# Ten warm-up operations for twelve, the layernorm's shift in one VectorE operation, and a new order table

## The chip, the cores and the metric

The kernel runs on one core of one Trainium2 chip. A core has five engines that work side by side, each with an instruction queue of its own: TensorE (PE; its weight loads are listed as PEld), VectorE (DVE), ScalarE (ACT), GpSimd (POOL) and SyncE (SP), which here issues nearly all transfers. The metric is the device time of one execution in microseconds, as a median of runs.

## The reference

Four residual blocks follow each other: attention, MLP, attention, MLP. S is 2048, D is 512, 32 heads of 16 columns, a sliding window of 256 keys, F is 1792.

```python
def _A_ref(x, wqkv, wo):                       # x already layernormed
    q, k, v = ...                              # x @ wqkv, 32 heads of 16
    scores = einsum("bhqd,bhkd->bhqk", q, k) * (Dh ** -0.5)
    scores = where((q_idx - k_idx >= 0) & (q_idx - k_idx < 256), scores, -1e9)
    return reshape(einsum("bhqk,bhkd->bhqd", softmax(scores), v)) @ wo

def _B_ref(x, w1, b1, w2, b2):                 # mixes along the tokens
    h = _layernorm(x)
    u = gelu(einsum("bsd,sf->bdf", h, w1) + b1)
    return transpose(einsum("bdf,fs->bds", u, w2) + b2)

x = A_x
x = x + _A_ref(_layernorm(x), A_wqkv, A_wo)
x = x + _B_ref(_layernorm(x), B_w1, B_b1, B_w2, B_b2)
x = x + _A_ref(_layernorm(x), A_wqkv, A_wo)
x = x + _B_ref(_layernorm(x), B_w1, B_b1, B_w2, B_b2)
```

## The kernel before

Everything stays in SBUF in bf16: x as 16 tiles of 128 tokens by 512 columns (`x_sb`), its normalised copy (`xh_sb`), and k, v and q of the stretch in work. A layer's attention runs over four quarters Q of 512 queries; in each, over four groups t of eight heads, and in each of these over nine steps m. A step multiplies q by k into two PSUM banks (`emit_scores`, L797), takes the exponential on ScalarE (L808), masks the edges of the window on VectorE or POOL (L825), and multiplies by v into banks 4 and 5 (`emit_pv`, L846). Between the steps stand the jobs that feed them: transposes of normalised tiles into `xhT` (L569, L582), projections for k, q (L593) and v (L697, turned on VectorE at L700, spread at L712 or L717), evacuations of PSUM by `copy_out` (L442 on VectorE, L444 on ScalarE), and the output projection (L762), after which x is added and its statistics are taken (L766, L527, L528). The MLP follows: L609 (parts made ahead, beside attention) and L987 with the gelu at L994, then L1033 with the sum at L1037. Banks 6 and 7 serve all these jobs in turn.

`ln_stats` (L526) takes mean and variance of a tile. `ln_apply` (L530) makes the normalised tiles from them, mostly four tiles at once: `vare`, the variance plus epsilon (L537, VectorE); `rstd`, its power -1/2 (L539, POOL); `nmean`, the mean times -1 (L541, VectorE); `shift`, `nmean` times `rstd` (L543, POOL); and per tile x times `rstd` plus `shift` (L546 on VectorE or POOL, L549 on ScalarE). There are 17 such calls: two of two tiles at the start, and 15 of four.

The start: four loads of one x tile, then the weights; on POOL the identity matrix, the triangle `tri` and some constants; on VectorE the mask `edge`, eight small pieces made from `tri` (L490, L492), the columns `half` and `even`; three zero fills of `q_sb` (L495) on VectorE or POOL. Meanwhile TensorE multiplies the identity by itself, twice in a warm-up operation (L521), into banks 4 and 5. Then tiles 0 to 3 are normalised, transposed, and multiplied into the first k, q and v. wv is also reordered in halves (`permute_wv`, L686 to L688).

The order of every engine is fixed beforehand. Each operation is registered with the engines that could take it, a priority and an estimate of its duration. A planner, `arrange`, could order them by these, but it isn't called as long as `LINES` is there: `given` takes each engine's list of operation numbers from that table, and with it the choice of engine. `ORDER` sets in which order the jobs are registered, and so who waits for whom; `BANKS` says which of banks 6 and 7 a job takes. An engine works its list strictly in order, and a wait at its head holds all behind it:

```python
    def emit(self, block):
        line = self.line = self.given() if LINES else self.arrange()
...
                    for k, (sem, val) in waits.items():
                        if seen.get(k, 0) < val:
                            seen[k] = val
                            e.wait_ge(sem, val)
                    o.on[ename][1](e).then_inc(o.mark[0], 16 if o.dma else 1)
```

Of the kernel before, what the change touches and what calls it, by code (L numbers as in the profile page):

```python
# [14 lines left out]
WARM = 12  # L15
# [14 lines left out]
def _table(*text):  # L30
# [5 lines left out]
    'c-pO%NfLlC2n6Z*|D!$VA(pZwQ02iO5IRgWGvj$=s}a1_t)7LW%>DZDUfy1PqA2I%kl8c?b5B|cGg6XlcP%#(x1TjeVa`gOe{yPcK<L$?wAm@}'  # L36
    'VkysiU77XM`Cn79HbaE`*=AYKIH|352Ds;6D^<qc%}i^DBpz)O@D)yLnj()z{$97jIlPxA?E)0O0EP')
ORDER = _table(
    'c-jTQ17HvU00h8C*0OEeT()i7ww7(%wr$(CZSxKgh_DC-BLspY6ao+$$q^f25FX(W5)ly<5fB5B5g(Bd577||DG(D$5C;hn7YPsz8ITC6kqn8E'
    '6xp#48IclckPoSl4QY`HMUW1eksDc%9t{u$Igu4PPyl6+7rBrJg^?eDD2O^JijpXV;;4dRD31~-h0<t`%BYC4D2FDfh6<>ON~nr%sE*pGfm*1C'  # L40
    'uIPhCXo~unfVyaohG>jd7>O2WgJx)nb{K?CXpOe$fR5;lE|`lR=!Ny@hwd1Np6H8F7=XbThHVH!e+<QNOha#sz!)6D5RAuYjKeI9#bivyOiaWi'
    'Ou=-_!3@mCJj};gEW`pV#R)9OA}ql&ti&p;zz3|w2JFTfY{EKh#8xcE4s5}8?7~hw#%0{a9_+_Ktj1m(z-HXT5gf)boWe((!BL#YN!-9C9LH&#'
    '!$n*Lc?B164cGAlw{R1;aR+hu0Qd0-uka90@dPjM9Ix>b&+rzB_y+Is4quR*pYR=@@eO|vnqL9_#xI!v@E2kThGZIsWf(?aAWJYZgE2fKF)G6`'
    'fH7Esu^5HX8J9m1it!nfu^EpE8Jr22go&Ay$(WJRn35@&nyHwU*_e(Q7?GKoo|%}HjhKZwn4P(pn|V2ytyq)!nUjT>hxu5LMOc)DS%Ae^ip5xl'
    'l~|r7S(T+(ku_L_)mWC5S&Ow<opo8C^;m}u*?>*ioNd^WP1u3W*qWW$j&0eVo!F5**o{5ei(T1;ec7A+*^gs6h{M>J137|2IGm$6n%y~plNiLI'
    'oXU|L&xstv>72r8oW<E3$C;eRxm>{cT*yUS#-&`z6<ovRoWnlc#?{=-bzIMD+`!3P!d+a<jl9gOyuwx7#GAa%&Ai1M+`{eL!L8iMJ>1Lv+{cqV'
    '!Bf1z(>%^&yvU<G$0Iz$!#u!)Jj+8o&-=W@+q}a^e9Gs1$9sIhXMD&f{K&g}%ny9cmwdw)e8snX&)@vaPyE7f45LW;&Y%2B3;Mx7{L7U3MJc!v'
    '=pRFh3awxYp->8^hzhF+3a`wHtf-2q=n7C2MN@1QR9wYUd^J)WB~c=kR&~WwLZwk+C07d7Rc@tMDrHn!^-)%3S4(A3E@e?R<y2nfQGVr90Zmp1'
    '1*)*Rsf-G#go>+_%Bj36sfvOWL)BDKHC0(vRYSE@TlLjYO_Wac)LadeT8-6AEtE;EltanXRPEG8om5h-)m3d(K^@gaWz|!iRZRU<RK3+h1Jz4|'
    ')mOtbK!Y??b<|!XHA15_R!cQn<FsEhH9_MwMUym7(==7nHACGsOS3gs{k2eYG+&FgM9XwktF%%pv|KwiTx+yi>oi6iwN@LnS?je;o3vFsG*R2N'  # L50
    'OIx%@yR}ybbWlfhSjTlpr*uN6bxy~0QfG8t7j;3G^iEH;NY`~)w{=6ebWL}3RrmBn4|P`dO+D8GJ<=Op(FfhvK0Vemeb!sO)_eWXC;ie_z0`O8'
    '(@%ZTU(tVbS1<HR!3@hG9MT^Z%Ap<H-}GDI9N;((ba+R0SVwaNM{-0*bxg;0DJODVM{#_|a6;#B7{_uF$8!QFcVZ`VN~dyCr*L$qab;(87N>So'
    'cXd{0a4u(dI%ju!_jev=b0ODuPUm(}7jy|1aWQ9d8K-qg=XC{_c6nEHK38%z7jR+Ma9P)NRTp;^S9cvZa6>nC6PI&KH+O5davQgEdv|ax_iz{2'
    'bA5MmH#c%m_jNP(a$65}9}jepTX=*Ad6<WKxJP@G$9s%BySFF0pT~KEC%L<)d9tT_fM<E8XLzpXc)pkWh>v-J7kagidaB2Ih}ZbAr+ATPdx=l@'
    'lo$J?k9&oedYM;xmDhT`*Lj0?dY5;5kN0|;cX+G!d!sk`kT-j~xA=hf`Jm7EhR^$wullra`i^h;uJ8G*&-sEc`nF&Aim&;)pZl`!`;i~}i68ix'
    'pZcL+`KA8@K7;B`')
# [80 lines left out]
class Plan:  # L137
# [1026 lines left out]
```

## Time and profile before

| | us |
|---|---|
| median of three runs (495.0, 495.05, 496.42) | 495.05 |
| the profiled execution | 497.66 |
| its span, first to last instruction | 495.9 |
| what lies around the span | 1.76 |
| TensorE busy in the span | 472.4 |
| first transposes of tiles / first scores | 9.47 / 15.26 |
| first layer's attention, about | 15 to 166 |
| first layer's MLP, about | 166 to 231 |
| second layer's attention, about | 231 to 406 |
| second layer's MLP to the end, about | 406 to 496 |

A row of the timeline is start, duration, engine, line, operation, result and sources, and in brackets the idle time before it with what ended it. A row of groups has, after the shapes and the count, the busy time in us and the mean of one in ns, then the engine's idle time before it. The granted clock of TensorE is 1.00 throughout; a second, lower rate shows only in the spacing of the first warm-up products.

### The profile page before, as it was taken

How to read it: one execution, taken by the hardware profiler on the slowest of the kernel's cores; microseconds unless marked ns; L12 is line 12 of the kernel's file. 1: busy time of each engine (PE TensorE's matmuls, PEld its weight loads, DVE VectorE, ACT ScalarE, POOL GpSimd, SP SyncE). 2: the span in 40 equal slices, each digit the busy share in tenths (PEclk: the TensorE clock that was granted, in tenths of full speed). 3: DMA queues.
4: the chain of work that ended last, by engine and by line, in shares of the span. 5: the costliest groups of instructions: out<-in, count | busy, mean ns of one | idle time of the engine just before them, and what ended most of it. 6: DMA issues, size and time to landing. Idle time of an engine off the chain costs nothing.

```text
span 495.9 us, 19594 instructions
## 1 busy us (share of the span) xinstructions
PE 472.4 (95%) x8478; PEld 272.3 (55%) x8550; DVE 325.5 (66%) x661; ACT 320.6 (65%) x392; POOL 211.4 (43%) x372
## 2 busy tenths in 40 slices
PE   8899999999989999999999998998999999999997
PEld 3455566554767444445555875666557654444444
DVE  7999888977763763357895467976996557331222
ACT  3899999998989403502977779889899941340000
POOL 5889546564664310002676445467475411100000
PEclk9999999999999999999999999999999999999999
DMA  6732212131413631331101321024233464040651
GB/s 211 76 99 82 73 55 82 62 99 43 122 56 114 196 106 58 91 98 52 33 18 42 112 79 48 5 75 140 80 91 109 136 189 130 10 138 33 203 169 63
DMA packets 78597, 45.58 MB, mean 92 GB/s; under 512 B 9008, under 2 KB 77488, under 8 KB 78512
## 3 DMA queue, kind: packets, MB, share of 16 engines
q1 hardware_dynamic: 74640, 44.32, 30.4%
q0 software_dynamic: 3872, 0.02, 1.3%
q8 instruction: 67, 1.10, 0.9%
q14 instruction: 18, 0.15, 0.1%
HBM read 33.56 MB, written 2.10 MB: 72 GB/s over the span
## 4 chain that ended last, share of the span: by engine, by line
PE 78%; DVE 9%; ACT 5%; issue 4%; DMA 2%; SPq 2%; POOL 1%; DVEq 0%; ACTq 0%; POOLq 0%
PE ps L1033 14%; PE ps L987 13%; PE ps L609 12%; PE ps L797 10%; PE ps L846 9%; PE ps L593 7%; PE ps L762 5%; ACT p_sb L808 4%; PE ps L697 4%; PE ps L521 2%; SPq L436 2%; PE ps L889 1%; DMA oU<-o 1%; DVE p_sb L825 1%; DVE vt L700 1%
## 5 line engine op out<-in xcount | busy, mean ns | idle before, releaser
L808 ACT ACTIVATE p_sb<-ps 128x1024 bf16<-128x1024 f32 (+8 forms) x288 | 261.4, 975 | 28.7 <-PE ps L797 24.8
L825 POOL TENSOR_TENSOR p_sb<-p_sb,edge 128x256 bf16<-128x256 bf16 (+2 forms) x266 | 131.2, 499 | 111.7 <-ACT p_sb L808 97.8
L797 PE MATMUL ps<-q_sb,k_sb 64*64 64x288 bf16 (+8 forms) x2816 | 107.9, 249 | 4.5 <-ACT p_sb L808 4.3
L846 PE MATMUL ps<-p_sb,v_all 64*34 64x288 bf16 (+17 forms) x2816 | 89.1, 245 | 1.8 <-DVE p_sb L825 0.8
L797 PEld LDWEIGHTS ps<-q_sb,k_sb 64*64 64x64 bf16 x2816 | 59.1, 106 | 51.4 <-ACT p_sb L808 23.7
L846 PEld LDWEIGHTS ps<-p_sb,v_all 64*34 64x34 bf16 (+1 forms) x2816 | 60.6, 100 | 12.1 <-issue 3.6
L593 PE MATMUL ps<-xhT,wqkv 128*128 128x512 bf16 x212 | 55.3, 380 | 4.1 <-issue 3.0
L539 POOL TENSOR_TENSOR rstd<-vare,mhalf 128x4 f32<-128x4 f32 (+1 forms) x17 | 16.6, 976 | 81.0 <-DVE vare L537 57.3
L825 DVE TENSOR_TENSOR p_sb<-p_sb,edge 128x128 bf16<-128x128 bf16 (+2 forms) x134 | 35.5, 279 | 20.3 <-ACT p_sb L808 18.0
L1037 DVE SCALAR_TENSOR_TENSOR x_sb<-ps,b2col,x_sb 128x512 bf16<-128x512 f32 x23 | 17.0, 748 | 43.3 <-PE ps L1033 42.7
L527 DVE BATCH_NORM_STATS2 stats<-x_sb 128x6 f32<-128x512 bf16 x64 | 42.7, 681 | 0.6
L609 PE MATMUL ps<-xh_sb,w1low 64*64 64x512 bf16 x640 | 41.7, 377 | 0.1
L634 DVE TENSOR_TENSOR k_sb<-ps,half 128x1024 bf16<-128x1024 f32 (+1 forms) x31 | 36.5, 1176 | 5.5 <-PE ps L593 5.0
L549 ACT ACTIVATE xh_sb<-x_sb,shift,rstd 128x512 bf16<-128x512 bf16 x12 | 9.5, 812 | 45.2 <-POOL shift L543 29.4
L1033 PE MATMUL ps<-ubuf,w1buf 128*128 128x512 bf16 x165 | 37.2, 379 | 0.2
L712 POOL TENSOR_TENSOR v_all<-vt,even 128x1024 bf16<-128x1024 f32 (+2 forms) x22 | 33.0, 1504 | 5.0 <-DVE vt L700 2.7
L1033 PE MATMUL ps<-ubuf,oU 128*128 128x512 bf16 x149 | 34.3, 379 | 0.3
L994 ACT ACTIVATE ubuf<-ps,b1col 128x512 bf16<-128x512 f32 x28 | 18.5, 686 | 23.9 <-DVE ps L992 20.0
L697 PE MATMUL ps<-xhT,wqkv 128*128 128x512 bf16 x112 | 30.0, 380 | 3.7 <-issue 1.3
L593 PEld LDWEIGHTS ps<-xhT,wqkv 128*128 128x128 bf16 x240 | 19.4, 98 | 24.8 <-issue 4.2
L992 DVE TENSOR_TENSOR ps<-ps,ubuf 128x512 f32<-128x512 f32 x20 | 14.0, 699 | 26.5 <-PE ps L987 26.4
L762 PE MATMUL ps<-wo_sb,oT 128*128 128x512 bf16 x117 | 29.4, 380 | 1.7 <-issue 0.8
(93 smaller groups left out, 545.5 us busy)
## 6 DMA issues: line engine op xcount, KB each, us to landing
w1buf<-in_B_w_dram SPq DMA_DIRECT2D x30, 256.0 KB
w1buf<-in_B_w_dram SPq DMA_DIRECT2D x42, 128.0 KB
w1low<-in_B_w_dram SPq DMA_DIRECT2D x40, 128.0 KB
oU<-in_B_w_dram SPq DMA_DIRECT2D x18, 256.0 KB
oU<-o SPq DMA_DIRECT2D x16, 256.0 KB
q_sb<-qt SPq DMA_DIRECT2D x120, 32.0 KB
xhT<-in_B_w_dram SPq DMA_DIRECT2D x4, 512.0 KB
k_sb<-in_B_w_dram SPq DMA_DIRECT2D x4, 512.0 KB
```

Of the source, the lines that this page charges most:

```text
L527: dve(lambda e: e.bn_stats(stats[:, t, :], x_sb[:, t, :]), 690, prio, reads=[R("x", t)], writes=[R("stats", t)])
L593: last = e.matmul(ps[:, b, :], lhsT=wqkv[:, c, c0:c0 + P], rhs=xhT[:, buf, c, :], start=(c == 0), stop=(c == 3))
L609: last = e.matmul(ps[64 * h:64 * h + 64, banks[r ^ swap], :], lhsT=lhs(r ^ swap, c, rows, 64 * h), rhs=rhs(r ^ swap, c, rows), start=(c == ...
L634: return e.tensor_tensor(dst, src.unsqueeze(2).to_broadcast([P, n, 2, w]), mask[:].unsqueeze(1).unsqueeze(3).to_broadcast([P, n, 2, w]), o ...
L697: last = e.matmul(ps[:, b, :], lhsT=wv[:, c], rhs=xhT[:, buf, c, :], start=(c == 0), stop=(c == 3))
L762: last = e.matmul(ps[:, b, :], lhsT=oT[:, buf, t, i * P:(i + 1) * P], rhs=wo_sb[:, t, :], start=(t == 0), stop=(t == 3))
L797: last = e.matmul(ps[64 * c:64 * c + 64, 2 * half + r, 32 * i0:32 * i1], lhsT=k_sb[rows, ring, t, kb % 16, :], rhs=q_sb[rows, t, c, 32 * i ...
L808: exps[plan.job] = last_exp[0] = plan.op({ACT: (170 + int(2 * (512 - c0) * 0.84), lambda e: e.activation(p_sb[:, slot, :, c0:512], ps[:, 2 ...
L825: return e.tensor_tensor(v, v, g, op=ALU.mult)
L846: last = e.matmul(ps[64 * r:64 * r + w, B_O + (c ^ r), 32 * i0:32 * i1], lhsT=v_all[rows, pos - 32 * c:pos - 32 * c + w], rhs=p_sb[rows, s ...
L987: r = e.matmul(ps[:, b, :], lhsT=blk[:, sc - 8 * part, (ft % 2) * P:(ft % 2 + 1) * P], rhs=xh_sb[:, sc, :], start=(sc == 8 * part), stop=( ...
L1033: r = e.matmul(ps[:, b, :], lhsT=blk[:, turn[n], (st % 2) * P:(st % 2 + 1) * P], rhs=u_at(turn[n]), start=(n == 0), stop=(n == NFT - 1))
```

## The change

Three edits in the source, and the tables.

```diff
-WARM = 12
+WARM = 10
...
         for n in range(WARM):
-            pe(warm, 860 if n < 4 else 432, -7.2, reads=[R("ident")], writes=[BK(B_O), BK(B_O + 1)])
+            pe(warm, 860 if n < 7 else 432, -7.2, reads=[R("ident")], writes=[BK(B_O), BK(B_O + 1)])
...
-        nmean = sb("nmean", [P, NT], dt.float32)
...
-            dve(lambda e: e.tensor_scalar(nmean[:, sl], agg[:, sl, 0], -1.0, None, op0=ALU.mult), 160, prio,
-                reads=[R("agg", t) for t in ts], writes=[R("nmean", g)])
-            pool(lambda e: e.tensor_tensor(shift[:, sl], nmean[:, sl], rstd[:, sl], op=ALU.mult), 200, prio,
-                 reads=[R("nmean", g), R("rstd", g)], writes=[R("shift", g)])
+            dve(lambda e: e.scalar_tensor_tensor(shift[:, sl], agg[:, sl, 0], -1.0, rstd[:, sl], op0=ALU.mult, op1=ALU.mult), 190, prio,
+                reads=[R("agg", t) for t in ts] + [R("rstd", g)], writes=[R("shift", g)])
```

The numbers 860, 432 and 190 are the planner's estimates in ns; with the tables given they set nothing. How the first loads and fills were reckoned when the new tables were made does not stand in the source; only the tables tell it. `BANKS`, `ORDER` and all five lists of `LINES` are replaced. They are compressed lists of numbers; unpacked and set against the operations, they say:

| list | operations before | after |
|---|---|---|
| TensorE | 1012 | 1010 |
| VectorE | 661 | 655 |
| ScalarE | 382 | 371 |
| POOL | 368 | 368 |
| SP | 377 | 377 |

At the start:

- SP: tile 3 of x is loaded before tile 2; all else to the eighth load as before.
- POOL: `tri` before the identity; two of the three zero fills of `q_sb` (one before); the ones in v's table (L512) ahead of the first `rstd`; two of the halves of wv (one before 16 us, two in all, before; four after).
- VectorE: one zero fill (two before), then all eight pieces of `edge` before the first statistics (five before); the first `vare` stands behind the statistics of all four tiles (behind those of two before); then the first shift, tile 0, the second shift, tiles 3 and 2, and only then the copy of the first transposed tile. The statistics of tiles 4 to 7 come before the first turn of v, not after it.
- ScalarE: one of the four first tiles (two before); both halves of the first q are masked here (on VectorE before).
- TensorE: nine warm-up operations, transposes of tiles 0 and 1, the tenth, transposes of 3 and 2. After the first k and q it projects the second q, where it projected the first v.

In the first layer's attention the ScalarE list loses two copies of transposed pairs, two q copies (and gains one), two PV copies, two v operations, one copy of `rc` and one half of wv, and one application of the layernorm goes and two come. VectorE and POOL have these in its place. TensorE's list keeps its stages, with neighbours exchanged; it passes between matmuls of 64x64 cells and full ones 198 times (200 before).

More of the change, by code (lines that the diff above doesn't have):

```diff
@@ L35 @@
 BANKS = _table(
[L36 to L37 removed]
+    'c-pm<;SK{K2!r`}|A*d|EV<;aBE=1ViGomDjrbVv5s?w!+0&FydG)?%MpvsGoTOqfqH>X`ldtD@Dx<NJvW6^U7^BDdb};T4(S_=$_I3Eg0;!Oh'
+    'DOYog?>WD(SRM#CYNO30x9&Xb)K%~ui964-eJVfVv#xLUBIXulhWv3}ezwY(vU;s>25j;bj>YU0zrug?-LV%0SO9?')
 ORDER = _table(
[L39 removed]
@@ new lines @@
+    'zNL5mi3{+-zO}FC+xigS(ZA+9`OdzJ@9w+$P~XG1_dR`>@8$dWNZ;2-_%xsBQ+=|}^cg<eFZ8)S#~1of{5rqK@9;<bXa0oW?~DC8f5Bh%m;Fz^'
+    '%-{0=1GaEMbN'),
+    "scalar": _table(
+    'c-jTQ31}8%7y#h!J-_$;Y}ATBF|``YB%3wN%4LEvktvobX&G#kl&iV2(mZ0Vwv_Df7*m|(M5rOUWYdXDSNfC1O3{%@%wsiZKXl+qa%Dot^V||j'
+    '!t^jR%n4h=BVlgX7oH2t!|S0wbcBszbLbAup(V72if}Nrg%jcPkPW@zbjXGN@O$_r01Sn{!}X8{x59831LL3=?t=!H0%b56%Hdh4f|p<xz6z_L'
+    '4pzhaum+l78+;6{uopU^3%-UPI17C+0KdWzTm?eI;W!ElaV!?$1iT;T;CyVsr|=m(gD>FAxC(3WU0jcwaR+{a?f5Ak!LRTbp2Q3IBmRb$@hT$a'
@@ new lines @@
+    'jFAkPB{{M{@}xitWr^f#iR_hwvQ<t?g_KE5YUG|glDG0%zDTpQ(T-Xq>!nzFYl^1n2py@T^|=1k$+}cm=sI1myL7jfYn4{(ZM~!QdRHIlEB&Qp'
+    'Vy!G{aTagwtwaxKAKS0}t)G=@v2CzSn{GKa*H+tF+hp5pm+iMwJ7VQ_$}ZUzyKVQZ-k#eFduJc)wSBh+<IrSrp<9R#JwvZBDs%_~LrRzuvO;!P'
+    '9E!rmuss|IN5koGE>wm)p*B1TPs5wg6uyM-0U|yk5sP$*q(=S&o@Tl&'),
+    "sync": _table(
+    'c-jTQNo)vc6ae7=z4!m`fA0-q4JBGKiBO}K;$m8K2qM~Qt7s&g%!P}HQ4S8aw&+1?>rhm!?bw3WHkoOQnMy2^s5TMQ91we5EY<oxaL$oK7o2zO'
+    'qTB9@-8NU^cDO=U;r@01xD&3~-F9{Eo>O2Dh+xp=zPfKN17<*{>voAS6H?(9D2H8826JI2tb`4)1&W~vwn7P1LI=Eq5AYr?Kr`Hc255ptXopTn'
@@ L122 @@
+    '7FfRJS+4E0GTUqWtlTQB)N1XVU9xJcv4eKhj@cnQW#_HZ{<Ld$-5RXU&RV_Qv}XIy?pT|(*dzN67xKM4'),
 }
```

141 lines of the change are left out of this document (65 added, 76 removed).

## The prediction

> **What bounds the kernel now.** I read first the page's busy times and its chain of waits.
>
> ```profile
> span 495.9 us, 19594 instructions
> ...
> PE 472.4 (95%) x8478; PEld 272.3 (55%) x8550; DVE 325.5 (66%) x661; ACT 320.6 (65%) x392; POOL 211.4 (43%) x372
> ...
> PE 78%; DVE 9%; ACT 5%; issue 4%; DMA 2%; SPq 2%; POOL 1%; DVEq 0%; ACTq 0%; POOLq 0%
> ```
>
> TensorE carries 78% of the chain and idles 23.5 us (495.9 - 472.4). So the useful question is where those microseconds lie. I asked for the busy time by stage. From 166 to 226 us and from 406 to 486 us (the two MLPs) PE is busy 19.5 to 19.95 of every 20 us: nothing to win there. Layer 0's attention, 16 to 166 us, is different:
>
> ```profile
> 16.00:26.00 10.00, 9.35 (x158) 4.62 (x159) 9.76 (x24) 9.19 (x14) 8.29 (x19) 1.00 1.02 116
> 26.00:46.00 20.00, 18.77 (x342) 10.31 (x345) 19.22 (x51) 18.75 (x28) 18.00 (x36) 1.00 0.29 88
> ...
> 86.00:106.00 20.00, 18.89 (x475) 11.12 (x471) 16.41 (x30) 19.54 (x22) 11.31 (x17) 1.00 0.25 71
> ...
> sum 150.00, PE 140.68 PEld 87.58 DVE 118.84 ACT 140.95 POOL 95.16; mean PE 17.59 PEld 10.95 DVE 14.85 ACT 17.62 POOL 11.90
> ```
>
> The columns after the length are the busy time of PE, weight loads, DVE, ACT and POOL. ACT (140.95 of 150) is as full as PE (140.68): two engines take turns as the bound, and DVE is full too until 46 us. The waits of PE agree; of whole-run waits the largest is:
>
> ```profile
> PE ps L797 <- ACT p_sb L808: 4.3, 7, 1.2
> PE ps L593 <- issue: 3.0, 19, 0.2
> ```
>
> The scores (L797) wait for the exponential (L808) to free a bank. Asked by window, 1.1 us of this lies in 16 to 100 us and 1.6 us in 100 to 170 us: 2.7 us in layer 0.
>
> **The start, and its two edits.** The timeline of the first 16 us:
>
> ```profile
> 1.70 8.15 PE L521 MATMUL ps<-ident 128*128 128x512 bf16 x24 [1.70 <-POOL ident L465]
> 1.91 0.95 POOL L495 MEMSET q_sb<- 128x1024 bf16 x1
> 2.12 0.81 DVE L490 COPY edge<-tri 32x32 bf16<-32x32 bf16 x1
> 3.27 0.17 DVE L490 COPY edge<-tri 32x32 bf16<-32x32 bf16 x1
> 3.97 1.28 DVE L527 BATCH_NORM_STATS2 stats<-x_sb 128x6 f32<-128x512 bf16 x2
> 8.67 0.79 DVE L546 TENSOR_SCALAR xh_sb<-x_sb,rstd,shift 128x512 bf16<-128x512 bf16 x2 [0.44 <-POOL shift L543]
> 10.85 0.61 PE L569 MATMUL ps<-ident,xh_sb 128*128 128x128 bf16 x8 [0.56 <-DVE xhT L442]
> 15.26 0.62 PE L797 MATMUL ps<-q_sb,k_sb 64*64 64x288 bf16 x16
> ```
>
> Weight loads of the warm-up are 0.43 us apart for 14 matmuls and some 0.2 us apart for the last ten: the first 14 run at the low rate, so all four matmuls that go are quick ones, 4 x 0.21 = 0.85 us. Today they do cost: the first normalised tile is there by some 8.4 us (ACT L549, 7.57 + half of 1.52) and the first transpose loads its weights at 9.47, when the warm-up lets go. If the warm-up were all that moved, the start would win up to 0.85 us.
>
> It is not. The new table reorders VectorE, and I chain it from rows. Before the first statistics stand one zero fill (0.48), all eight edge operations (0.205 apart, from the starts 3.07, 3.27, 3.48, 3.68) and some fills of `even` (0.1 each). `tri` is made first, ready by 1.5 instead of 1.9. So the statistics begin at s = 1.6 + 1.64 + 0.4 = 3.6, against 3.97 now, **if nothing blocks**. But two fills of 0.95 now stand on POOL, beside these copies. The rows show the price: the copy at 2.12, beside POOL's fill from 1.91 to 2.86, took 0.81 us and ended 0.07 after it; its twin at 3.27 took 0.17. That is 0.64 us for one block, so s is 3.6, 4.25 or 4.9 with none, one or two.
>
> [...]
>
> From s: four statistics 2.6, four aggregates 0.5, both `half` 0.3, `vare` 0.17 (now behind the last statistics, earlier behind the second), a hop of 0.1 between engines (POOL's shift ended at 7.47, ACT began at 7.57) and `rstd` 0.72 twice, the second shift 0.19, two applications 0.87 and the copy of the first transposed tile 0.42, which stands behind them in VectorE's queue: s + 6.6, and the second pair of transposes 0.15 later. That gives 10.35, 11.0 or 11.65, where the trace has 10.85: -0.5, +0.15, +0.8. From there to the first scores it takes 4.41 now (15.26 - 10.85). In the new table ScalarE carries it: to the copy 0.42, copy 0.60, hop 0.1, mask 0.84, a reordering of weights 0.41, two masks 1.68, the change to scores 0.42 (PEld's idle time before L797): 4.47. I take **+0.2 us** for the start, one block, with -0.5 and +0.9 as ends. The warm-up's 0.85 us is hidden behind this chain.
>
> **The layernorm's shift.** Off VectorE goes `nmean`, off POOL the product; on VectorE comes one operation with two SBUF inputs, which no row shows.
>
> ```profile
> L539 POOL TENSOR_TENSOR rstd<-vare,mhalf 128x4 f32<-128x4 f32 x15 | 15.2, 1011 | 78.5 <-DVE vare L537 54.9 <-DVE nmean L541 23.4
> L543 POOL TENSOR_TENSOR shift<-nmean,rstd 128x4 f32<-128x4 f32 x15 | 3.3, 220 | 1.7 <-DVE nmean L541 0.5
> ```
>
> `nmean` takes 157 ns (its row) and `vare`, the nearest in shape, 202; I take 190 (ends 157 and 220). 17 x 0.03 = 0.6 us more on VectorE, 17 x 0.22 = 3.7 us less on POOL, which is not the bound. The chain `rstd` to `shift` to application is as long as before. What is new is a wait: VectorE now stands at `shift` until POOL's `rstd` is done, and masks, casts and PSUM evacuations are queued behind it. Cover is the VectorE work that the table puts between `vare` and `shift`. Of the 15 later layernorms five have 1.9 us or more, six have 1.16 to 1.36, one has 0.35, and three have none. With POOL free the wait is 1.2 minus the cover (1.01 plus two hops of 0.1): 0.85 for the one, 1.2 for each of the three, which lie in the MLP stages, where VectorE is busy 9 to 15 of 20 us. With one POOL mask of 0.685 (L825's row) ahead of `rstd`, the six would wait some 0.64 each and the one 1.5: 5.4 us. VectorE is 79% busy in attention (118.84 of 150), so at most 4.3 us reach the path; below, 0.5 us of PE waits on `nmean` can vanish. I take **+0.1 us**, nearest to POOL being free: in attention POOL is busy 95 of 150.
>
> **The new table's placement.** By the unpacked lists ScalarE loses in layer 0's attention: two copies of transposed pairs (2 x 1.029), one q copy net (0.600), two PV copies (2 x 0.607), two v operations (two passes of 0.40, two of 0.75: 2.3), one `rc` copy (0.322) and one weight reordering (0.414), and gains one application (0.812) and loses one (0.812): 2.06 + 0.60 + 1.21 + 2.3 + 0.32 + 0.41 = 6.9; one more application falls in front (tile 4), so net 6.1 us of 141. VectorE takes 0.68 for each such copy, but the statistics of tiles 4 to 7 (4 x 0.68 at 16 to 20 us now) move ahead of the first scores, so the full stretch to 46 us is not made fuller; later VectorE has 3 to 9 us free in 20. In layer 1 ScalarE loses only some 2 us. TensorE's order changes in neighbours (200 changes between matmul kinds become 198), not in amount.
>
> A lighter ScalarE shortens PE's waits for the exponential. Bounds: 0, and all 9.3 us that PE idles from 16 to 166 us (150 - 140.68). Nearest are the 2.7 us of waits that name L808; 6.1 us taken away is more than twice that, but scattered, so I take **-2.2 us**. Next late is PE itself. The loads of w2 for the last MLP stand in another order; the tightest pair has 6.9 us from the release of its place to its use by planned PE work, against 7.3 now, with no PE wait today: nothing. The tail (last product, sum, store) is unchanged.
>
> **Sum.** +0.2 + 0.1 - 2.2 = -1.9 us. Against the profiled execution's 497.66 us (span 495.9) this is 495.8; that execution stands 2.6 us above the median 495.05, so by the median 493.2 us.
>
> **Rivals.** (1) *No gain*: PE bounds layer 0 after all, and ScalarE's 6.1 us become its own idle time; for it PE's 19.53 of 20 us at 146 to 166, against it ACT's 19.54 at 86 to 106. Only start and shift are left: +0.3, so 495.4, or 496.1 with two blocks. (2) *Slower*: VectorE held by POOL at `shift` in attention. It decides once a POOL mask stands ahead of `rstd` in most of the six covers of 1.2 us, so that they wait; price 0.7 (0.85 x 0.79) to 4.3 us, middle 2.5. As VectorE also took over ScalarE's copies, the relief of -2.2 is then not seen: 495.05 + 0.2 + 2.5 = 497.8. For it speak 19.22 of 20 us of VectorE at 26 to 46 us; against it that its waits on POOL's `shift` are only 4.7 us today. [...]
>
> **How the numbers follow.** Forecast (493.2, alone 490.8 to 494.9) 0.47, no gain 0.27, slower 0.26. About 0.3%, or 1.5 us, is what a measurement of this kernel tells from no change. Of the forecast 0.06 falls inside that; of no gain 0.23 inside and 0.03 above, 0.01 below; of slower 0.24 above, 0.02 inside: faster 0.42, same 0.31, slower 0.27. The forecast's lower end is the start at -0.5 and a relief of 3.7 (0.4 of the idle 9.3). Range 490.8 to 498.4, the slower case with the start at its upper end, 0.9 in place of 0.2.
>
> **What would show it.** Start: the copies beside POOL's fills at 0.8 us or 0.17; the second transposes at 11.0; scores at 15.5. Relief: ACT busy near 135 in layer 0's attention and PE's wait on the exponential under 1.5 us. Shift: VectorE waits on POOL's `rstd` under 4 us in all. I am wrong if PE's idle time in 16 to 166 us does not fall, or if the exponentials wait longer for scores because VectorE is late.

## The result

The changed kernel takes 502.76 us as a median (500.04 to 504.11), the kernel before 495.31 us beside it (495.0 to 496.42): a ratio of 1.0142, with a 95% interval of 1.0112 to 1.0172. Forecast was 493.2 us. Two more measurements of the changed kernel and of a control that should equal it, both below, give 1.0086 and 1.0102, so the loss is 4 to 7 us. The profiled execution of the changed kernel took 500.04 us and is the shortest of its set; the rest of the loss is in executions without a profile. Its granted clock of TensorE is 1.00, but four of the other five have 0.993 to 0.997; the last section comes back to this. In this kernel the line numbers of the body are lower by two to four; in the kernels of the experiments they move by some lines more.

The page of the changed kernel, its span, busy times and the engines of its chain:

```profile
span 498.3 us, 19554 instructions
...
PE 472.0 (95%) x8475; PEld 274.4 (55%) x8546; DVE 335.3 (67%) x655; ACT 316.2 (63%) x381; POOL 213.8 (43%) x372
...
PE 73%; DVE 11%; issue 7%; ACT 4%; POOL 2%; DMA 2%; SPq 1%; POOLq 0%; DVEq 0%; ACTq 0%
```

TensorE's work is the same (472.0 us, 472.4 before), so what was lost is idle time: 26.3 us against 23.5. In the chain TensorE fell from 78% to 73%, and "issue", time for which the profile shows no cause, rose from 4% to 7%. The busy times in layer 0's attention (length, PE, PEld, DVE, ACT, POOL):

```profile
16.00:26.00 10.00, 9.06 (x149) 4.59 (x151) 9.91 (x25) 9.54 (x16) 9.42 (x16) 1.00 1.01 104
26.00:46.00 20.00, 18.55 (x345) 10.24 (x349) 19.65 (x47) 17.55 (x25) 17.46 (x35) 1.00 0.29 85
...
86.00:106.00 20.00, 18.86 (x476) 11.27 (x476) 16.25 (x26) 19.46 (x21) 13.32 (x22) 1.00 0.26 74
...
sum 150.00, PE 140.45 PEld 88.15 DVE 123.33 ACT 138.41 POOL 98.83; mean PE 17.56 PEld 11.02 DVE 15.42 ACT 17.30 POOL 12.35
```

ScalarE is lighter by 2.5 us (140.95 before), yet TensorE idles 9.55 us here, as much as before (9.32). Its waits over the whole run:

```profile
PE ps L842 <- issue: 2.3, 3, 1.0
PE ps L589 <- issue: 2.2, 14, 0.2
...
PE ps L793 <- ACT p_sb L804: 1.4, 5, 0.5
...
PE ps L842 <- DVE o L440: 0.7, 1, 0.7
```

The wait of the scores for the exponential fell from 4.3 to 1.4 us: the relief came, in the size forecast. In its place stand three waits of the product with v (L842) of up to 1.0 us for "issue", which the kernel before does not have on this line at all. The start, from the timeline:

```profile
1.55 2.86 DVE L488 COPY edge<-tri 32x32 bf16<-32x32 bf16 x4
1.92 0.96 POOL L493 MEMSET q_sb<- 128x1024 bf16 x1
2.84 0.96 POOL L493 MEMSET q_sb<- 128x1024 bf16 x1
5.57 0.69 DVE L525 BATCH_NORM_STATS2 stats<-x_sb 128x6 f32<-128x512 bf16 x1
10.60 1.57 DVE L542 TENSOR_SCALAR xh_sb<-x_sb,rstd,shift 128x512 bf16<-128x512 bf16 x2
11.07 0.95 POOL L1067 MEMSET spread<- 128x1024 bf16 x1 [0.70 <-DVE xh_sb L542]
12.55 0.62 PE L565 MATMUL ps<-ident,xh_sb 128*128 128x128 bf16 x8 [0.88 <-DVE xhT L440]
16.43 0.62 PE L793 MATMUL ps<-q_sb,k_sb 64*64 64x288 bf16 x16 [0.28 <-ACT q_sb L635]
```

The statistics begin at 5.57 (3.97 before; forecast 3.6 to 4.9), the second transposes at 12.55 (10.85; forecast 11.0) and the scores at 16.43 (15.26; forecast 15.5): the start lost 1.17 us. The four edge copies take 2.86 us where four take 0.8 alone, since two fills stand beside them, and two applications take 1.57 us beside a third fill where two took 0.79 before.

### The profile page after: what moved, and what is told of

Read it like the earlier page. It is cut to its first block, busy times and chain, and to the rows that moved or that the text cites. A ratio compares the mean times of both kernels' runs of the same rounds, so it can differ in the third digit from the quotient of the medians.

```text
span 498.3 us, 19554 instructions
## 1 busy us (share of the span) xinstructions
PE 472.0 (95%) x8475; PEld 274.4 (55%) x8546; DVE 335.3 (67%) x655; ACT 316.2 (63%) x381; POOL 213.8 (43%) x372
## 4 chain that ended last, share of the span: by engine, by line
PE 73%; DVE 11%; issue 7%; ACT 4%; POOL 2%; DMA 2%; SPq 1%; POOLq 0%; DVEq 0%; ACTq 0%
PE ps L1029 14%; PE ps L983 10%; PE ps L605 10%; PE ps L793 10%; PE ps L842 9%; PE ps L589 7%; PE ps L758 5%; PE ps L693 4%; ACT p_sb L804 3%; DVE stats L525 2%; DVE p_sb L821 1%; DVE xh_sb L542 1%; PE ps L885 1%; POOL p_sb L821 1%; SPq L434 1%
## 5 line engine op out<-in xcount | busy, mean ns | idle before, releaser
L804 ACT ACTIVATE p_sb<-ps 128x1024 bf16<-128x1024 f32 (+7 forms) x288 | 261.5, 972 | 33.2 <-PE ps L793 27.7
L821 POOL TENSOR_TENSOR p_sb<-p_sb,edge 128x64 bf16<-128x64 bf16 (+2 forms) x281 | 137.5, 497 | 110.4 <-ACT p_sb L804 96.8
L793 PE MATMUL ps<-q_sb,k_sb 64*64 64x288 bf16 (+8 forms) x2816 | 109.3, 249 | 2.7 <-ACT p_sb L804 1.4
L842 PE MATMUL ps<-p_sb,v_all 64*34 64x288 bf16 (+17 forms) x2816 | 90.1, 245 | 4.1 <-issue 2.3
L793 PEld LDWEIGHTS ps<-q_sb,k_sb 64*64 64x64 bf16 x2816 | 61.6, 106 | 44.8 <-ACT p_sb L804 20.6
L842 PEld LDWEIGHTS ps<-p_sb,v_all 64*64 64x64 bf16 (+1 forms) x2816 | 61.1, 100 | 17.5 <-issue 7.5
L605 PE MATMUL ps<-xh_sb,w1low 64*64 64x512 bf16 x640 | 42.6, 377 | 0.1
L708 POOL TENSOR_TENSOR v_all<-vt,even 128x1024 bf16<-128x1024 f32 (+2 forms) x20 | 30.5, 1533 | 2.2 <-DVE vt L696 1.9
```

The source lines that it names most:

```text
L605: last = e.matmul(ps[64 * h:64 * h + 64, banks[r ^ swap], :], lhsT=lhs(r ^ swap, c, rows, 64 * h), rhs=rhs(r ^ swap, c, rows), start=(c == ...
L793: last = e.matmul(ps[64 * c:64 * c + 64, 2 * half + r, 32 * i0:32 * i1], lhsT=k_sb[rows, ring, t, kb % 16, :], rhs=q_sb[rows, t, c, 32 * i ...
L804: exps[plan.job] = last_exp[0] = plan.op({ACT: (170 + int(2 * (512 - c0) * 0.84), lambda e: e.activation(p_sb[:, slot, :, c0:512], ps[:, 2 ...
L821: return e.tensor_tensor(v, v, g, op=ALU.mult)
L842: last = e.matmul(ps[64 * r:64 * r + w, B_O + (c ^ r), 32 * i0:32 * i1], lhsT=v_all[rows, pos - 32 * c:pos - 32 * c + w], rhs=p_sb[rows, s ...
```

## The experiments

Four theories stood at the start. **A**: the start loses. **B**: VectorE waits at the shift. **C**: the new order of the engines' work costs in attention itself. **D**: it leaves the on-chip moves less slack. A fifth, **E**, came out of the traces of the first eight. Lists are told as diffs of one engine's order.

**Parts alone.** First the kernel before with ten warm-ups, then with the shift in one operation, its place in VectorE's list where `rstd` was done in the profile.

```diff
-WARM = 12
+WARM = 10
```

> The kernel before with ten warm-up operations in place of twelve, the last two dropped, all else in the old order. Theory A (the changed kernel loses in its start: first tiles late, TensorE idle before the transposes, its clock not held) makes this kernel tell how much of it the warm-up count is: if ten are too few for the clock, 497 to 500 us with spread between runs; if the count is harmless, 494.6 to 495.3, since the transposes begin up to 0.8 us earlier. Theory B (the shift on VectorE waits for GpSimd) and theory C (the new placement in attention) give 495 +- 0.8.

```diff
-            dve(... nmean ...)
-            pool(... shift <- nmean * rstd ...)
+            dve(lambda e: e.scalar_tensor_tensor(shift[:, sl], agg[:, sl, 0], -1.0, rstd[:, sl], op0=ALU.mult, op1=ALU.mult), ...
```

> The kernel before with the one-operation shift on VectorE in place of nmean and GpSimd's product, put into VectorE's old order where the trace of before has rstd done. Theory B: 498 to 502, with VectorE waits on rstd of 4 us and more. Theories A and C: 494.5 to 496, since the chain from rstd to the normalised tiles is as long as before.

Measured: 0.9987 (0.997 to 1.0004) and 0.9996 (0.9971 to 1.002). The first exponential came 1.3 us earlier with ten warm-ups, but the median did not follow. Neither part costs anything by itself. That speaks against B, though the shift's place here was chosen so that it waits little; in the changed kernel VectorE waits 3.9 us in all for `rstd`, 3.4 of them in the MLP stages and none in layer 0's attention.

**The new order with the old start, and the changed kernel again.**

```diff
 every engine's list of the changed kernel, but up to the first scores
-the start of the changed kernel, ten warm-ups
+the start of the kernel before, twelve warm-ups
```

> The changed kernel, shift on VectorE and all, but with the start of before up to the transposes of the first four tiles: twelve warm-up operations in a row, one zero fill on GpSimd and two on VectorE, the first variance behind two statistics, two of the first tiles normalised on ScalarE. Theory A: 495 to 497.5 and no more spread between runs than before. Theories B and C: 501 to 504, as the changed kernel.

> The changed kernel again, for its spread between runs (500.0 to 504.1) and for a second profile. Theory A: runs differ by the time at which the clock of TensorE reaches its full rate or falls back, the profile of a longer run shows slow matmuls between 8 and 25 us. Theories B and C: the same clock in all runs, and the differences lie in attention.

Measured: 1.0046 (1.0019 to 1.0073) and 1.0086 (1.0054 to 1.0118). The difference, about 2 us, goes to the start (A), as an estimate, since the two intervals overlap; 2.3 us (0.9 to 3.6) are left for the order of the rest, which was forecast to win 2. The sign that the second expectation names for A, a clock that falls back, is there in some executions: 6 of the 10 have a granted clock of 0.990 to 0.997 (last section).

**More places for the moves.** In both kernels `qt` gets a third place, and `o2` two more in the idle MLP buffer.

```diff
-        qt = sb("qt", [P, 2, 512])
+        qt = sb("qt", [P, 3, 512])
...
-                copy_out(o2[:, k, :], ps[:, B_O + 1, :], B_O + 1, prio, 680, [R("o2", k)])
+                po, keys = (o2b, ...) if t0 and (prio < 380 or Q == 3) else (o2, ...)
+                copy_out(po[:, k, :], ps[:, B_O + 1, :], B_O + 1, prio, 680, keys[k])
```

> The changed kernel with its own tables, and more places for the on-chip moves: q's pieces (qt) have three places, not two, and o2 four, not two, wherever the MLP's buffer is idle (all of layer 0, the last quarter of layer 1); the triangle and a scratch column lie in that idle buffer too. No operation is added, left out or reordered, so only waits for the landing of a move can go. Theory A (the start) explains 1.6 of the loss and is untouched here. Theory D, the new order leaves the moves of q and o2 less slack, and what they land late stalls TensorE: the changed kernel falls from about 501 to 498.0-498.8 us and its runs lie closer together (within 3 us). Theory C without D (TensorE loses by the order of the engines' work itself): 500.5-501.5, as wide as now (up to 7 us).

> The kernel before with the same added places. D: the old order had slack, so 0 to -0.7 us (495.7-496.4). If it wins as much as the changed kernel does, 2 us or more (494.4 or less), the moves' places bound both orders alike and do not explain the difference. C: no statement, 496.4 within 0.7.

Measured: 1.007 (1.0044 to 1.0097) and 0.9992 (0.9976 to 1.0008). A gain of some 0.8 us for the changed kernel lies inside the intervals, and its executions still spread over 6 us: D is at most a small part.

**One layer each.**

```diff
 all lists: start and layer 1 of the kernel before
-layer 0 of the kernel before
+layer 0 of the changed kernel
```

> Start of before with twelve warm-ups, the shift in one operation, the changed kernel's order and engines for all other work of layer 0, and those of the kernel before for layer 1. The two layers together (new order, old start) cost +2.3 us (+0.9 to +3.6). C and D, spread evenly over both layers: +1.1 us, 497.5. If layer 0 alone carries it: 498.7, and layer 1 alone then nothing. The prediction's relief of ScalarE (-2.2 us, in layer 0) would show here alone: 494.2.

> The converse: start and layer 0 in the order of before (with the shift in one operation), layer 1 in the order and on the engines of the changed kernel. C and D spread evenly: +1.1 us, 497.5. If layer 1 alone carries the loss: 498.7. If layer 0 carries it: 496.4. By the prediction's terms layer 1 has no relief of its own and no loss: 496.4.

Measured: 1.0027 (1.0002 to 1.0051) with the new layer 0, 1.0044 (1.0021 to 1.0068) with the new layer 1. Both lose; there is no one bad stage.

**What the traces then showed.** Each matmul record was set against the operation that issued it. TensorE's long "issue" gaps lie *inside* operations, where this kernel puts no wait (`emit` sets them ahead of an operation): here, in a control run described below, between the 7th and the 8th of the twelve matmuls of one L852 (the product with v):

```profile
379.84 0.37 PE L852 MATMUL ps<-p_sb,v_all 64*34 64x128 bf16 x7 [0.26 <-POOL p_sb L831]
382.12 0.31 PE L852 MATMUL ps<-p_sb,v_all 64*64 64x288 bf16 x4 [1.90 <-issue]
```

The page's list of DMA queues (packets, MB, share of the engines) has one of the kind "instruction":

```profile
q1 hardware_dynamic: 74640, 44.32, 30.2%
...
q8 instruction: 67, 1.10, 0.9%
```

67 packets of 16,384 bytes, and TensorE has 8546 pairs of weight load and matmul: 127.6 pairs to a packet. I took each packet for a block of TensorE's own instructions; that is concluded from these numbers and the ones that follow. The halts stand at fixed numbers of TensorE's stream, whatever operation is there, and end 1.25 to 1.45 us after a q8 packet has landed (worked out from the traces; in brackets the halt in us between two weight loads, then the time from the landing to the next weight load):

```
weight load at which TensorE goes on
ten warm-ups alone      2761 (0.66, 1.40)  3016 (1.03, 1.39)
changed kernel          3017 (1.01, 1.25)  3527 (0.75, 1.39)  6445 (1.19, 1.45)  6572 (0.71, 1.40)  7335 (1.02, 1.40)
changed, old start      3017 (0.52, 1.27)  7335 (1.87, 1.33)  7970 (1.12, 1.44)
```

The spacing is 127 or a multiple of it to within two. So at the end of a block TensorE halted here where the next one was late. The packet starts 0.65 us (median, kernel before) after the block ahead of it was entered and takes 0.9 to 1.6, and in the halts above TensorE went on 1.25 to 1.45 us after the landing: by these numbers, as an estimate, a block that TensorE works off in less than some 3 us (0.65 + 0.9 + 1.25) halts it in any case. In the new order short matmuls (scores, products with v, the 32 of L885) stand closer together at the ends of three blocks: the 22nd (which ends at weight load 3017), the 43rd and the 49th, counted from 0 by the packet that is fetched meanwhile, take 2.9, 3.1 and 2.8 us without the halts at their ends, and 4.2, 5.2 and 4.2 in the kernel before. And the packet can start late. Over 677 blocks of eleven profiles, the longer the start was delayed, the more data the 16 DMA engines moved meanwhile:

```
delay of the packet, us          blocks   data moved meanwhile, us per engine
under 0.25                          108   0.01
0.5 to 0.75                         109   0.13
1 to 1.5                            152   0.43
2 to 3                               30   1.58
over 3                                6   2.98
```

Gaps between weight loads inside operations up to 410 us, counted from 0.25 us, sum to 0 us in the kernel before and 5.0 in the changed one; the other kernels of the old order have 0 to 2.2, the others of the new order 2.2 to 4.6. TensorE's idle time is shorter, 3.6 us for these 5.0, as its matmuls outlast their weight loads (245 ns on average against 100 at the product with v). This is theory **E**.

The kernel before is not free of it. The 4.2 us of its 22nd block end with its longest wait for the exponential, 1.16 us at weight load 3016, the same end of a block at which the kernel with ten warm-ups halts; without this wait the block takes some 2.7 us. The exponential had ended 0.54 us before these scores start, where after five of the other six waits of this kind they follow 0.05 us behind it, and they start 1.33 us after a packet landed. So some 0.5 of the 4.3 us that the profile puts down to the exponential, by estimate, were a halt too, at the head of an operation, where it can't be told from a wait.

**One load moved.** The longest halt in most profiles of the new order, in the pv of quarter 3, group 1, step 4 of layer 1, has a 512-KB load just ahead of its packet.

```diff
 SP's list of the changed kernel, layer 1
+288a w1more
 ...
 300  w1buf
-301  w1more
 302  w1low
```

> The changed kernel with one entry of SP's list moved: the 512-KB load of w1more in layer 1 is issued 12 places (9 us) earlier, where the kernel before has it. Theory E: TensorE's instructions come in 16-KB packets over the same DMA engines (queue q8, 67 packets); a packet that stands behind a bulk load lands late, and TensorE halts inside an operation until 1.4 us after it has landed. In every profile of the new order it halts 1.0 to 1.9 us in the pv of (quarter 3, group 1, step 4) of layer 1, and there the packet stands behind this load. E: this halt goes or falls under 0.4 us, the packet starts within 1 us of the block before it being entered (now 1.7 to 3.1), and the kernel gains 1.0 to 1.6 us: about 500.3 where the changed kernel has 501 to 502.8. Theory C (the order of the engines' own work): the halt stays, 501 to 502.8.

```diff
 SP's list of the kernel before, layer 1
-288  w1more
 ...
 300  q_sb<-qt
+300a w1more
 301  w1buf
```

> The converse: the kernel before with the same load moved 13 places later, to 0.3 us ahead of where TensorE enters the block of instructions whose successor is fetched there (374.8 us). E: a halt inside an operation appears near 378 us, 1 to 1.9 us long, and the kernel loses 1.0 to 1.6 us: 497.5 to 498.1 against 496.5. C, or if the load's place is of no account: no halt, 496.5 within 0.7.

Measured: 1.0108 (1.0073 to 1.0144) and 1.001 (0.9989 to 1.003). Both expectations of E failed. In the first the halt stayed (0.98 us): the packet now started 3.0 us after the block was entered, behind pieces of q and two w1buf loads. In the second no halt of 0.45 us appeared. So this load by itself is not the cause.

**Thin loads.**

```diff
-            load(w1low[:, fb % 2, 2 * j:2 * j + 2], w1v[:, 2 * j:2 * j + 2, ...
+            n = P if prio < 380 else 8
+            load(w1low[:n, fb % 2, 2 * j:2 * j + 2], w1v[:n, 2 * j:2 * j + 2, ...
```

> The changed kernel with the loads of w1 in layer 1 (w1low, w1buf, w1more and the four homes of the rest) cut to 8 of 128 partitions; the second MLP therefore multiplies mostly weights that lie there from before. All instructions, waits and issues stay. E: the halts of layer 1 (2.3 to 3.3 us in the profiles of the new order) go, those of layer 0 (1 to 2.2 us) stay: -2.3 to -3.0 us, 498.5 to 499.5. C: no more than the kernel before gains by the same cut.

> The kernel before with the same cut of the layer 1 loads of w1. E: its profiles show no halt over 0.4 us in layer 1, so 0 to -0.7 us: 495.8 to 496.5. C and E differ in the difference of the two cuts: E gives the changed kernel 1.6 to 3 us more than this one, C nothing.

Measured: 1.0046 (1.0027 to 1.0065), against 1.0108 for its neighbour with all loads, and 0.9975 (0.9956 to 0.9994). The cut gives the new order 3.1 us and the old one 1.2: the difference of 1.9 us is in E's range, but it hangs on that neighbour (by the changed kernel's own ratios of 1.0086 and 1.0142 it would be 0.8 and 3.5). But in layer 1 a halt of 0.76 us was left, with next to no load about: the close order can suffice.

**Only the blocks' ends moved.** Added pairs in the warm-up shift all later instructions, and nothing else.

```diff
+        def pads(count):
+            def f(e):
+                for n in range(count):
+                    r, c = n // 2 % 2, n % 2
+                    rows = slice(64 * r, 64 * r + 64)
+                    last = e.matmul(ps[64 * c:64 * c + 64, B_O + r, 0:32], lhsT=ident[rows, 0:64], rhs=ident[rows, 0:32], ...
+                return last
+            return f
+        PADDED = {8: 94}
...
-            pe(warm, 860 if n < 7 else 432, ...
+            pe(pads(PADDED[n]) if n in PADDED else warm, 860 if n < 7 else 432, ...
```

> The changed kernel with 92 more pairs of weight load and product (64x64 weights, 32 columns, some 14 ns a pair) in the ninth warm-up operation, where TensorE waits for the first normalised tile anyway. Nothing else changes; every later instruction of TensorE stands 184 places later in its stream. The halts seen so far stand at the same numbers of that stream whatever operation is there (2762, 3017, 3527, 6445, 7335, ... weight loads, about 127 apart or a multiple of it), so the blocks' boundaries now fall on other operations. From the spacing of the loads in the profiles of the new order, a boundary moved by 84 to 96 loads leaves a third of the shortfall (0.7 in place of 2.1 us by the mean delay). Theory E: the halts of 3.7 to 5.2 us fall to 1 to 2, and the kernel gains 2 to 3 us: 499 where it has 501 to 502.8. Theory C or the loads' places alone: 501 to 502.8, with the halts at the same operations as before.

> The kernel before with 62 such pairs in place of its last two warm-up operations (four pairs), which takes the same time: 116 instructions more. By the same reckoning the old order stands at its best place now (0.8 us) and near its worst with 58 loads more (2.0 us). E: halts of 1.5 to 3 us appear in attention, and the kernel loses 1.2 to 2.5 us: 498 to 499 against 496.6. C: 496.6 within 0.7.

> Control for the first: the changed kernel with 128 pairs more, one whole block of 256 instructions, so that the boundaries fall on the same operations as without them. E: the halts stay at the operations and at the size that the changed kernel has (3.7 to 5.2 us), 501 to 503. If pairs at the start gain by themselves, it falls as the first does.

> The new order of all work behind the start, with the start of before (twelve warm-ups, of which the last three hold 98 pairs in place of six). Without the pairs this kernel has 1.0046 of the time before. E: with the boundaries moved its halts fall from 4.3 us to about 1.2, and what is left is the relief of the waits on the exponential (2 us): 495.0 to 496.5, the only one of these that could beat the kernel before. C: 1.0046 again, 498.9.

Measured: 1.0041 (1.0019 to 1.0062) with 92 pairs, 1.0102 (1.0074 to 1.013) with 128. The intervals are apart: the place of the blocks' ends is worth 0.6%, 2.8 us, though in the profile with the 92 pairs the first exponential came 1.2 us later (its granted clock was 0.50 for 3.4 us just before, see the last section). The difference stays when executions of like clock are compared: 497.9 against 501.1 us with a clock of 0.999 or more (means of 4 and 3), 499.4 against 502.5 with less (8 and 3). One thing is not held apart: the profile with 128 pairs has a mask held behind POOL in layer 0 that the one with 92 has not (last section). With 128 pairs the halts stand in the same four operations as in the changed kernel, at numbers 128 higher (3145, 3655, 6573, 7463); with 92 those of layer 0 are gone and 2.2 us are left. With the old start and 98 pairs for six, 1.0009 (0.9994 to 1.0023), where the same kernel without them had 1.0046; that is a little more than E expected, and a part may be the clock's, which was granted in full in all 12 executions with the pairs and in 5 of 10 without. The held mask can't be the reason here, as the profile with the pairs has it and the one without has not. The old order with 58 pairs, however, took 0.9982 (0.9966 to 0.9998): halts of 0.71 and 0.80 us did appear in layer 1, but the loss did not. Its wait for the exponential fell from 4.3 to 2.2 us meanwhile, so these halts took the place of waits; a halt is not always a loss of its length.

**The fills moved.** POOL's list in the start, then the same with 92 pairs.

```diff
 POOL's list of the changed kernel
-q_sb fill, tmp, q_sb fill, tmp, tmp, ones, rstd, rstd, spread fill, spread, wv, ones
+tmp, tmp, tmp, ones, q_sb fill, q_sb fill, rstd, rstd, wv, ones, spread fill, spread
```

> The changed kernel with POOL's list reordered in the start alone: the two zero fills of q_sb come behind the first ones of v (so after VectorE's edge pieces, ahead of rstd), and the fill and first select of spread come behind the first reordering of wv and the second ones of v. Theory A: VectorE's first edge copy takes 2.27 us because it stands locked through both fills, and the two applications beside the spread fill take 1.57 in place of 0.85; with the fills moved the copy takes 0.17, the statistics begin near 3.5 (now 5.57), and the first exponential comes at 14.3 to 15.2 us (now 16.9, and 18.0 in three profiles). The kernel gains 1.5 to 2.5 us: 499.3 to 500.3 where the changed kernel has 501 to 502.8. If the start is hidden later (as the 1.3 us were that ten warm-ups gained alone): 501 to 502.8. The halts stay as they are.

> Both causes taken away: the fills moved as in the run before it, and 92 more pairs of weight load and product at the start (two warm-up operations replaced by 96 pairs), which moves the boundaries of the instruction blocks as before. If A and E are the whole loss: 498.8 (with the pairs alone) less 1.5 to 2.5 for the start, so 496.3 to 497.3, the same as the kernel before within 0.2%. If something else costs too, it stays above 498.

Measured: 1.0063 (1.0036 to 1.0089) and 1.0031 (1.0011 to 1.0051). The start of the first:

```profile
1.55 1.04 DVE L486 COPY edge<-tri 32x32 bf16<-32x32 bf16 x4
3.75 0.69 DVE L523 BATCH_NORM_STATS2 stats<-x_sb 128x6 f32<-128x512 bf16 x1
4.98 1.83 POOL L491 MEMSET q_sb<- 128x1024 bf16 x2
8.79 0.74 DVE L540 TENSOR_SCALAR xh_sb<-x_sb,rstd,shift 128x512 bf16<-128x512 bf16 x2
13.78 0.62 PE L791 MATMUL ps<-q_sb,k_sb 64*64 64x288 bf16 x16 [0.27 <-ACT q_sb L633]
```

The copies take 1.04 in place of 2.86 us, the applications 0.74 in place of 1.57, and the scores come 2.65 us earlier. The time gained by it is smaller and not sharply known, 1.1, 1.9 or 3.9 us by the ratios of the changed kernel and of its control (1.0086, 1.0102 and 1.0142). In this profile the lead is gone by 50 us: the first v now waits 1.16 us for POOL's wv, and at 42.6 us a mask stands for 1.93 us behind POOL (last section). With both causes taken away 1.5 us (0.5 to 2.5) stay over the kernel before, a little more than expected. What they are is not settled; halts of 1.4 and 0.7 us inside operations are still in that profile, as are four held masks and a stretch of half clock (last section).

## Why the prediction was wrong, step by step

- **The step that failed** is the one behind the relief of ScalarE: "Next late is PE itself." The relief was right as a wait (scores on the exponential: 4.3 to 1.4 us; under 1.5 forecast), but next late was not TensorE's work: by theory E it was TensorE's supply of instructions. From 16 to 410 us its waits on ScalarE fell by 3.0 us (5.2 to 2.2), and those with no releaser rose by 3.3 (5.6 to 8.9). In layer 0 alone, 16 to 166 us, those on ScalarE fell by 1.8 (3.2 to 1.4), those with no releaser rose by 0.9 (3.2 to 4.1) and those on VectorE by 1.2 (2.3 to 3.5). The sign named for being wrong came true: the idle time there did not fall. The prediction shows the row of "issue", whose pieces are 0.2 us in the kernel before, and draws nothing from it; it took "200 changes between matmul kinds become 198" for an unchanged order of TensorE, and did not count how many short matmuls stand between two packets.
- **VectorE's share**, the work taken over from ScalarE, was put at nothing, as VectorE "has 3 to 9 us free in 20". Its busy time in layer 0 rose by 4.5 us (118.84 to 123.33), and free time on average did not help: most of the rise is four masks that stand behind POOL (last section).
- **The 2.7 us** that the relief was sized by were not all the exponential's: some 0.5 of them, by the estimate above, were a halt for instructions, which a lighter ScalarE can't shorten.
- **ScalarE's 6.1 us** were too many: its busy time fell by 2.5 us, not 6, to 138.4 and not 135. The 6.1 were added up from durations, which overlap: those of the operations that start from 16 to 166 us sum to 152.9 us, with ScalarE busy for 140.95. By that sum it lost 4.4 us, as two weight reorderings (0.84) and one more exponential (0.45) came into this stretch.
- **The start** was mis-sized: +0.2 us taken, +0.9 as the end, 1.17 measured. I priced a blocked copy at one fill (0.64 us) and two at twice that. In fact one copy stood through both fills (2.27 us), as the second fill began before the first had ended. The block at the third fill (0.8 us on the two applications) was missing: I set the application at its unblocked duration while POOL's `spread` fill moved beside it. With the fills moved the four copies took 1.04 us and the two applications 0.74.
- **The warm-up** was right: ten alone, 0.9987 (0.997 to 1.0004).
- **The shift** was right, in mechanism too: alone it is 0.9996, its long waits lie in the MLP stages as said, and in the changed kernel VectorE waits for `rstd` less than the 4 us named:

```profile
DVE shift L539 <- POOL rstd L537: 3.9, 4, 1.1
```

- **The rivals.** The slower one had VectorE held by POOL, as happened, but in the wrong place (at the shift, not at the masks). The case "no gain" was nearest, as TensorE's idle time in layer 0 stayed the same, but for another reason. That the time could lie above 498.4 us was in none of the cases.
- **The best execution against the median.** The prediction compares a profile with a profile (497.66 and 500.04), while the medians are 7 us apart: the new order's executions spread over 4 to 9 us, those of the old one over 4. The last section shows two differences between them that were seen, a held mask and the granted clock; neither was tried as a cause.

## What to carry to other kernels

Count TensorE's instructions, not only its microseconds: where a block of some 127 short matmuls with their weight loads took less than about 3 us (2.8 to 2.9 where it halted), or the next packet started late, it halted for its own code here, as theory E reads the traces, and the waits that were removed came back as "issue". This kernel puts no wait inside an operation, so look for halts there; the queue of instruction packets in the profile, set beside the gaps, shows it, and a few added instructions at the start (or a control with a whole block, here 128 pairs) tell a bad place of the blocks' ends from a bad order. And work on POOL was not free here: what VectorE copied beside a fill waited for its end (a copy of 0.17 us took 0.81), and for the end of the next one too where that started before (2.27). Look at the granted clock of every execution, not only of the profiled one.

## What the runs showed that was not expected

The place of the blocks' ends is worth some 0.6% of this kernel, by the two runs with pairs, so two orders differ in part by luck: any change of TensorE's instruction count in front moves it.

VectorE's masks can be held in mid-attention as its edge copies were at the start, and in the two profiles below whether they are hangs on 0.05 us. In the changed kernel, measured again, four masks end before POOL spreads v (L708):

```profile
43.47 0.75 DVE L821 TENSOR_TENSOR p_sb<-p_sb,edge 128x64 bf16<-128x64 bf16 x4
...
44.11 1.89 POOL L708 TENSOR_TENSOR v_all<-vt,even 128x1024 bf16<-128x1024 f32 x1
```

In the control with 128 pairs POOL began 0.05 us earlier:

```profile
43.52 2.51 DVE L831 TENSOR_TENSOR p_sb<-p_sb,edge 128x64 bf16<-128x64 bf16 x4
...
44.06 1.90 POOL L718 TENSOR_TENSOR v_all<-vt,even 128x1024 bf16<-128x1024 f32 x1
```

The last mask then stood until POOL was done: the four took 2.51 us in place of 0.75, and the exponentials from 50 to 118 us are 1.4 to 1.9 us later than in the other execution. Of the eleven profiles with the whole new order five have this (their executions took 498.0 to 502.7 us); six, the fastest of 496.92 us among them, do not (496.9 to 500.0).

Four more masks stand behind POOL's spreads of v between 50 and 102 us in every profile with the new layer 0, and in none of the kernel before's order. One of them in the changed kernel:

```profile
55.01 1.90 POOL L708 TENSOR_TENSOR v_all<-vt,even 128x1024 bf16<-128x1024 f32 x1
55.58 1.47 DVE L821 TENSOR_TENSOR p_sb<-p_sb,edge 128x256 bf16<-128x256 bf16 x1
```

The four take 5.3 us there, where masks of their shapes take 1.2 on average before, and each ends up to 0.15 us after the spread. They are a candidate for what stays over when both causes are taken away. All this was seen, not tried.

The granted clock of TensorE, taken over an execution, is below 0.999 in 9 of the 15 executions of the changed kernel that its two ratios rest on, and in 4 of 141 of the kernel before. The nine took 500.1 to 504.1 us (median 503.1), the six others 496.9 to 503.5 (median 499.8). Seven profiles show the cause of the lower figure, one stretch of 3.41 us at a granted clock of 0.50. Here it is with the 92 pairs (the granted clock is the third figure from the end):

```profile
10.00:12.00 2.00, 1.23 (x10) 0.56 (x10) 1.89 (x4) 1.39 (x2) 1.30 (x2) 1.00 0.16 53
12.00:14.00 2.00, 1.44 (x11) 1.29 (x12) 0.87 (x4) 0.60 (x1) 1.85 (x5) 0.54 0.00 0
14.00:16.00 2.00, 2.00 (x14) 1.49 (x12) 1.46 (x4) 1.17 (x4) 1.94 (x4) 0.61 0.00 0
```

In three profiles the stretch begins at 12.0 to 12.9 us, after TensorE had waited 2.4 us or more for the first normalised tile: the 16 products of the first k and q take 2.9 to 3.5 us there and 2.05 to 2.19 in the others, and the first exponential comes near 18.0 us, not 16.95. In three others it begins at 377 to 383 us, right after the longest halt (1.7 to 1.9 us), and in one at 17.3 us. With the 92 pairs TensorE was idle for some 2.1 of the 3.41 us ahead of it. In the profile of the changed kernel TensorE waited 1.6 us for the first tile and halted for up to 1.2, and its clock stayed at 1.00. So a late tile or a halt can cost up to 1.7 us of TensorE's work on top of itself (an estimate, half of 3.41), or nothing; what decides between the two was not shown. No run was made to try this, so how much of the loss goes this way stays open.
